# A fused attention and MLP kernel: more row transposes on SyncE's DMA queue, and the schedule around them shifted

## The chip, the cores and the metric

The kernel runs on one core of a Trainium2 chip. The metric is the device time of one execution in microseconds (us); lower is better. Three executions of the kernel before are given, and one more was profiled.

## The reference, cut to what matters

Eight batches, eight heads each, 576 positions, head width 64. Per head: causal attention with a decay bias that comes from a running sum over the positions. Then, per batch, the heads are laid side by side (512 columns), normalised and sent through an MLP with a residual.

```python
scores = q @ k.T / 8                              # causal, 576 x 576 per head
bias   = -(cum[:, None] - cum[None, :])           # cum = cumsum(max(s, 0))
attn   = softmax(where(causal, scores + minimum(bias, 0), -1e9))
x      = concat_heads(attn @ v)                   # (8, 576, 512)
xn     = (x - mean(x)) / sqrt(var(x) + 1e-6) * g_ln
out    = x + maximum(xn @ w_ch1, 0) @ w_ch2       # 512 -> 2048 -> 512
```

## The kernel before

**Order by hand.** Every engine executes its instructions in the order in which the program issues them. Batch 0 and the first heads of the next two batches follow a written plan (a long word list, not touched). From head 18 on a loop runs over the remaining heads: n counts all 64 heads, b = n // 8 is the batch, h = n % 8 the head in the batch.

**One head n.** `scores(b, h)` issues the score matmuls in three PSUM banks (sa, sb, sc; line 346), each followed by an exponential on ScalarE; GpSimd clears the part above the diagonal (line 366). Every second head adds the small last block (`scores_d`, line 382). `pv_next()` does attention times V (line 424) for the head issued two heads earlier, and VectorE normalises it.

**MLP units as filler.** Between these steps TensorE gets units of the MLP of the batch before, taken from the list `queue`. A chunk is one batch's MLP over 512 rows: 16 units of `mlp1` (line 538, four 128x512 matmuls each) and 16 of `mlp2` (line 556, the same size), 32 in all. A chunk ends at a fixed head (`end`), where the rest of the list is run and the next batch's 32 units are put in; its first unit is then issued behind the next head's scores. The number of units in a head is the rest of the list divided by the heads left. The fourth unit of each block of 128 rows is followed by VectorE's residual add (`yo`, line 565) and a store issued by SyncE (line 583).

**Rows of x.** In the heads h = 1 and 2 of batch b, `ln_xn` makes the normalised rows `xn` of batch b-1 on VectorE: four tiles of 128 rows, and for odd batches a fifth one that holds the 64 last rows of two batches. The MLP needs them transposed (xT, xTm). For b up to `NXD` = 6 that is done by `ln_tr` in the heads 2 and 3: four TensorE transposes per tile (line 526) into PSUM and a copy by VectorE or ScalarE. For b = 7 and at the end `ln_tr_dma` does it: one DMA transpose per tile, issued by SyncE (line 518).

**Rows of q and k.** A group `gam` is four heads; the even groups are the heads 0 to 3 of a batch, the odd ones 4 to 7. From group 5 on its k and q are loaded in five tiles of rows: two loads per tile issued by SyncE (`ld_rows`, line 175, into a staging pool of six), a cast with the bias columns on GpSimd (`cast_rows`, lines 192 and 195), and a DMA transpose per tile issued by SyncE (`tr_rows`, line 208) into one of two buffers `kq`. `pre(n)` and `post(n)` place these steps by m = n - 4 gam: loads at m = -6, -5, -4, casts at -5, -4, -3, transposes at -4 (tiles 0, 1) and -3 (tiles 2, 3, 4). The group's first scores are at m = 0.

**One queue.** All of SyncE's transfers stand in one order: stores, loads, transposes. An issue waits in that order for what it needs (the store for `yo`, a transpose for its cast or for `xn`), and everything behind it waits too.

Of the kernel before, what the change touches and what calls it, by code (L numbers as in the profile page):

```python
# [19 lines left out]
def kernel(  # L20
# [11 lines left out]
    nc = tc.nc  # L32
    B, H, S, D = q.shape
# [13 lines left out]
    G = 4  # L47
    NG = BH // G
    NPE = 5
    NM = 10  # L50
    NHW = 16
    NXD = 6
    KT = 96
    QT = 6
    QP = S // QT
# [103 lines left out]
    def ld_cast_pair(g):  # L159
        ld_cast("k", g)  # L160
        ld_cast("q", g)

    def ld_cast_v(b, t):
        pn = P if t < NF else TL
        nc.gpsimd.dma_start(  # L165
            out=v_bf[b % 2][:pn, t, :, 0:D],
            in_=v[b, :, t * P : t * P + pn, :].rearrange("h s d -> s h d"),
        )

    def ld_rows(gam, t):  # L170
        pn = P if t < NF else TL
        b, h0 = gam // 2, (gam % 2) * G
        tmp = stage.tile([P, 2, G, D], F32, name="rowtmp", tag="st")
        for u, src in enumerate((k, q)):
            nc.sync.dma_start(  # L175
                out=tmp[0:pn, u],
                in_=src[b, h0 : h0 + G, t * P : t * P + pn, :].rearrange("h s d -> s h d"),
            )
        loaded["rows", gam, t] = tmp

    def ld_cast_rows(gam, t):
        pn = P if t < NF else TL
        b, h0 = gam // 2, (gam % 2) * G
        for u, src in enumerate((k, q)):
            nc.gpsimd.dma_start(
                out=rows[t][0:pn, u, :, 0:D],
                in_=src[b, h0 : h0 + G, t * P : t * P + pn, :].rearrange("h s d -> s h d"),
            )
# [10 lines left out]
    def bias_of_rows(gam, t):  # L199
        pn = P if t < NF else TL  # L200
        nc.vector.tensor_copy(
            out=rows[t][0:pn, :, :, D:KA], in_=cT[0:pn, t, :, gam * G : (gam + 1) * G, :]
        )

    def tr_rows(gam, t):
        pn = P if t < NF else TL
        o = t * 2 * G * P
        nc.sync.dma_start_transpose(
            out=kq[home(gam)]
            .rearrange("p u h s -> p (u h s)")[:, o : o + 2 * G * pn]  # L210
            .rearrange("p (h s) -> p h s", s=pn),
            in_=rows[t][0:pn].rearrange("p u h c -> p (u h c)"),
        )
# [8 lines left out]
    def ld_w2(i):  # L222
        nc.gpsimd.dma_start(
            out=w2_bf[:, 4 * i : 4 * i + 4, :], in_=w2_r[:, 4 * i : 4 * i + 4, :]
        )
# [3 lines left out]
    def aug(gam, eng, h0=0):  # L229
        r = slice(gam * G + h0, gam * G + G)  # L230
        i = home(gam)
        eng.dma_start(out=kq[i][D : D + 1, 1, h0:G, 0:S], in_=c_hi[r, :])
        for j in range(3):
            eng.dma_start(out=kq[i][D + 1 + j : D + 2 + j, 0, h0:G, 0:S], in_=c3[r, j, :])
# [214 lines left out]
    def x_tiles(b):  # L449
        ts_ = [xb[b][:, t, :] for t in range(NF)]  # L450
        if b % 2 == 1:
            ts_.append(xm[b // 2])
        return ts_

    st = {}

    def ln_stats(b, part):
        if part == 0:
            st[b] = small.tile([P, 5, 3, 6], F32, name="stats", tag="stats", bufs=2)
        lo, hi = ((0, 256), (256, 384), (384, 512))[part]  # L460
        for t, x in enumerate(x_tiles(b)):
            nc.vector.bn_stats(out=st[b][:, t, part, :], in_=x[:, lo:hi])  # L462

# [8 lines left out]
    def ln_rstd(b):  # L474
        n = len(x_tiles(b))
        rs = rstd[:, b, 0:n]
        nc.vector.tensor_scalar_add(out=rs, in0=mvs[b][:, 0:n, 1], scalar1=1e-6)  # L477
        nc.gpsimd.tensor_tensor(out=rs, in0=rs, in1=mhalf[:, 0:n], op=ALU.pow)  # L478

    def ln_aggr(b, t):  # L480
        nc.vector.bn_aggr(out=mvs[b][:, t, :], in_=st[b][:, t, 0 : 2 if b == 0 else 3, :])

    def ln_xn(b, t):
        tiles = x_tiles(b)
        if t >= len(tiles):
            return
        if b == 0:
            nc.vector.tensor_scalar(
                out=mean0[:, t : t + 1],
                in0=sum0[:, t, 0:1],  # L490
                scalar1=sum0[:, t, 1:2],
                scalar2=1.0 / Dm,
                op0=ALU.add,
                op1=ALU.mult,
            )
        else:
            ln_aggr(b, t)
        xn = xnp.tile([P, Dm], BF16, name="xn", tag="xn")
        nc.vector.scalar_tensor_tensor(  # L499
            out=xn,  # L500
            in0=tiles[t],
            scalar=mvs[b][:, t, 0:1] if b > 0 else mean0[:, t : t + 1],
            in1=gb,
            op0=ALU.subtract,
            op1=ALU.mult,
        )
        xns[b, t] = xn
        if b > 0 and t == len(tiles) - 1:
            ln_rstd(b)

    def xT_dst(b, t):
        if t < NF:
            return xTs[b][:, :, t * P : (t + 1) * P]
        return xTm[:, :, (b // 2) * P : (b // 2 + 1) * P]

    def ln_tr_dma(b, t):
        if (b, t) in xns:
            nc.sync.dma_start_transpose(out=xT_dst(b, t), in_=xns.pop((b, t)))
# [78 lines left out]
    def run_units(n, dve_first=False):  # L597
        for i in range(n):
            if queue:
                first_unit[0] = dve_first and i == 0  # L600
                queue.pop(0)()

# [25 lines left out]
    for i in range(2):  # L630
# [8 lines left out]
        out=maskT,  # L639
        in_=maskT,  # L640
# [210 lines left out]


    def pre(n):
        if n in PAIR_LOADS:
            ld_cast_pair(PAIR_LOADS[n])
        if n in (11, 12):
            ld_w2(n - 9)
        if n in (8, 9):
            aug(n - 5, nc.sync)
        for gam in range(NPE, NG):  # L860
            m = n - 4 * gam
            ts_ = {-6: (0, 1), -5: (2, 3), -4: (4,)}.get(m, ())
            for t in ts_:
                if gam < NHW:
                    ld_rows(gam, t)
                else:
                    ld_cast_rows(gam, t)
                    bias_of_rows(gam, t)
            if gam >= NHW:
                for t in {-4: (0, 1), -3: (2, 3, 4)}.get(m, ()):  # L870
                    tr_rows(gam, t)
        for nb in range(2, B):
            t = n - H * nb + {2: 5, 3: 4}.get(nb, 6)
            if 0 <= t < NT:
                ld_cast_v(nb, t)

    def post(n):
        for gam in range(NPE, NHW):
            m = n - 4 * gam
            for t in {-4: (0, 1), -3: (2, 3)}.get(m, ()):  # L880
                tr_rows(gam, t)
            for t in {-5: (0, 1), -4: (2, 3), -3: (4,)}.get(m, ()):
                cast_rows(gam, t)
            if m == -3:
                tr_rows(gam, 4)

    def pv_next():
# [5 lines left out]
        if ph_ == 7:  # L893
# [6 lines left out]
            out=c_in[:, 0:P], in0=c_in[:, 0:P], scalar=0.0, in1=eight, op0=ALU.max, op1=ALU.mult  # L900
# [24 lines left out]
            out=c_in[:, P:S], in_=c_in[:, P:S], func=ACT.Relu, scale=1.0 / scale  # L925
# [44 lines left out]
    for word in PLAN.split():  # L970
        step, _, eng = word.partition(":")
# [2 lines left out]
        STEPS[name](*args, *([E[eng]] if eng else []))  # L974

    pend += [(2, 0), (2, 1)]
    FIRST = {24: 2}
    for n in range(2 * H + 2, BH):
        b, h = n // H, n % H
        pre(n)  # L980

        end = next(m for m in [8 * i + (3 if i <= NXD else 4) for i in range(2, B)] + [BH + 3] if m >= n)
        nu = -(-len(queue) // (end - n + 1)) - 2
        if n in FIRST:
            run_units(FIRST[n])
            nu -= FIRST[n]
        scores(b, h)
        run_units(1, True)
        if h % 2 == 0:
            scores_d(b, h // 2)  # L990
        post(n)
        run_units(1)
        pv_next()
        pend.append((b, h))
        if b <= NXD:
            if n == 2 * H + 2:
                for t in range(3, NT):
                    ln_xn(1, t)
            for t in {1: (0, 1, 2), 2: (3, 4)}.get(h, ()) if b > 2 else ():
                ln_xn(b - 1, t)  # L1000
                if t in (1, 2, 4):
                    run_units(1)
                    nu -= 1
            for t in {2: (0, 1), 3: (2, 3, 4)}.get(h, ()):
                ln_tr(b - 1, t, "act" if b == 2 else "dve")
                if t not in (1, 4) and nu > 0:
                    run_units(1)
                    nu -= 1
        elif h in (1, 2):
            for t in ((0, 1, 2), (3, 4))[h - 1]:  # L1010
                ln_xn(b - 1, t)
                ln_tr_dma(b - 1, t)
                run_units(1)
                nu -= 1
        run_units(nu)
        if n == end:
            run_units(len(queue))
            queue += batch_units(b - 1)
# [41 lines left out]
```

## Time and profile before

| | us |
|---|---|
| three executions: median (lowest, highest) | 357.67 (356.28, 358.16) |
| the profiled execution: its time | 357.56 |
| its span, first to last instruction | 355.8 |
| TensorE busy in the span | 347.7 (98%) |
| VectorE, ScalarE, GpSimd busy | 197.1, 185.6, 161.9 |
| mean granted TensorE clock | 1.000 |

The profiled execution lies 0.11 us under the median, and 1.8 us of its time lie outside the span. A line of the profile's groups reads: line of the kernel, engine, operation, written and read tiles and shape, count | busy time in us, mean ns of one | idle time of the engine just before, and what ended it. SPq rows are what SyncE issues; their duration is the time that the issue took, not the transfer. "<-" stands between what is written and what is read.

### The profile page before, as it was taken

Reading aid. Unit: us, or ns where it says so; the run is one execution under the profiler, and the core shown is the slowest. Engines: PE = TensorE matmul, PEld = TensorE weight load, DVE = VectorE, ACT = ScalarE, POOL = GpSimd, SP = SyncE. Lnnn points to the kernel's source line nnn. Section 1 sums busy time; section 2 is a strip of 40 time slices with the busy share of each in tenths; the row PEclk is TensorE's granted clock in tenths of the full one; section 3 lists DMA queues with packets and bytes.
Section 4 is the critical chain, followed back from the end, with each engine's and each line's share of the span. In section 5 each row is a group of like instructions: output and inputs, shape, how many; then the busy total and the mean of one; then the engine's idle time right before and its main releaser. Section 6 shows DMA issues by size and latency. Waiting matters only on the chain.

```text
span 355.8 us, 8451 instructions
## 1 busy us (share of the span) xinstructions
PE 347.7 (98%) x3170; PEld 199.3 (56%) x3170; DVE 197.1 (55%) x535; ACT 185.6 (52%) x359; POOL 161.9 (45%) x340
## 2 busy tenths in 40 slices
PE   7999998999999999999999999999999999999995
PEld 3899665555555555655555555555555544444444
DVE  7788877854277545944385548643664492113112
ACT  4899785577633773267435752476356502502500
POOL 9996578367366535583547354845341000000000
PEclk9999999999999999999999999999999999999999
DMA  9999999999999998799599958999650033011013
GB/s 150 173 172 161 202 192 171 160 223 162 179 189 199 175 210 113 156 209 186 112 189 182 198 117 150 216 173 175 133 129 2 0 73 121 0 61 60 0 32 89
DMA packets 169258, 49.73 MB, mean 140 GB/s; under 512 B 157776, under 2 KB 164608, under 8 KB 169216
## 3 DMA queue, kind: packets, MB, share of 16 engines
q1 hardware_dynamic: 116096, 36.53, 54.4%
q0 software_dynamic: 51600, 11.87, 37.4%
q10 hardware_dynamic: 1520, 0.79, 0.9%
q8 instruction: 25, 0.41, 0.5%
q14 instruction: 17, 0.14, 0.1%
HBM read 37.11 MB, written 9.44 MB: 131 GB/s over the span
## 4 chain that ended last, share of the span: by engine, by line
PE 83%; DMA 9%; SPq 3%; DVE 2%; ACT 2%; issue 0%; POOL 0%; DVEq 0%
PE py L556 31%; PE ph L538 31%; PE pot L424 6%; DMA v_bf<-in_v_dram 4%; PE sc L346 3%; PE sb L346 3%; PE sa L346 3%; DMA rowtmp<-in_k_dram 3%; SPq L175 3%; DMA kq<-c 2%; PE trx L526 2%; PE st L716 1%; ACT er L733 1%; PE trt L694 1%; DMA out_dram<-yo 1%
## 5 line engine op out<-in xcount | busy, mean ns | idle before, releaser
L556 PE MATMUL py<-w_bf,hT 128*128 128x512 bf16 (+2 forms) x608 | 135.6, 368 | 1.2 <-DMA w_bf<-in_moe_w_ch_dram 1.2
L538 PE MATMUL ph<-xT,w_bf 128*128 128x512 bf16 x480 | 113.3, 379 | 0.0
L548 ACT ACTIVATE hT<-ph 128x512 bf16<-128x512 f32 x101 | 60.2, 598 | 73.1 <-PE ph L538 73.1
L556 PEld LDWEIGHTS <-hT 128*128 128x128 bf16 x608 | 53.9, 98 | 51.3 <-issue 1.3
L366 POOL TENSOR_SCALAR_AFFINE_SELECT er<-er 128x256 bf16<-128x256 bf16 x108 | 44.9, 423 | 81.8 <-ACT er L357 80.8
L538 PEld LDWEIGHTS <-w_bf 128*128 128x128 bf16 x544 | 48.9, 98 | 49.2
L357 ACT ACTIVATE er<-sa 128x512 bf16<-128x512 f32 x56 | 33.4, 596 | 63.8 <-PE sa L346 47.7
L546 DVE TENSOR_SCALAR hT<-ph 128x512 bf16<-128x512 f32 x35 | 24.2, 692 | 56.6 <-PE ph L538 51.6
L346 PEld LDWEIGHTS <-kq 68*128 68x128 bf16 x412 | 29.5, 97 | 20.3
L424 PEld LDWEIGHTS <-er 128*128 128x128 bf16 x840 | 32.9, 98 | 12.4 <-issue 0.5
L565 DVE SCALAR_TENSOR_TENSOR yo<-py,rstd,xb 128x512 f32<-128x512 f32 x32 | 24.0, 749 | 28.6 <-PE py L556 20.6
L192 POOL CAST kq<-rowtmp 128x512 bf16<-128x512 f32 (+1 forms) x55 | 33.3, 606 | 8.7 <-DMA rowtmp<-in_q_dram 8.2
L424 PE MATMUL pot<-v_bf,er 128*128 128x65 bf16 x840 | 35.3, 193 | 0.5 <-DMA v_bf<-in_v_dram 0.4
L436 DVE RECIPROCAL rinv<-pot 128x5 f32<-128x5 f32 x56 | 10.7, 191 | 44.4 <-PE pot L424 44.3
L165 POOL DMA_DIRECT2D v_bf<-in_v_dram x40 | 34.5, 870 | 0.5 <-ACT er L357 0.3
L357 ACT ACTIVATE er<-sc 128x512 bf16<-128x512 f32 x56 | 34.2, 610 | 0.0
L357 ACT ACTIVATE er<-sb 128x512 bf16<-128x512 f32 x56 | 33.5, 598 | 0.0
L438 DVE TENSOR_TENSOR xb<-pot,rinv 128x256 f32<-128x256 f32 x56 | 23.8, 425 | 1.9
L478 POOL TENSOR_TENSOR rstd<-rstd,mhalf 128x4 f32<-128x4 f32 (+1 forms) x8 | 8.9, 1112 | 34.3 <-DVE rstd L477 34.3
L499 DVE SCALAR_TENSOR_TENSOR xn<-xb,mv,gb 128x512 bf16<-128x512 f32 x28 | 22.4, 800 | 1.0
L462 DVE BATCH_NORM_STATS2 stats<-xb 128x6 f32<-128x128 f32 (+1 forms) x84 | 21.9, 320 | 0.3
L346 PE MATMUL sc<-kq 68*128 68x256 bf16 (+1 forms) x200 | 21.7, 226 | 0.1
(115 smaller groups left out, 352.0 us busy)
## 6 DMA issues: line engine op xcount, KB each, us to landing
out_dram<-yo SPq DMA_DIRECT2D x32, 256.0 KB
rowtmp<-in_k_dram SPq DMA_DIRECT2D x44, 128.0 KB
rowtmp<-in_q_dram SPq DMA_DIRECT2D x44, 128.0 KB
v_bf<-in_v_dram POOLq DMA_DIRECT2D x32, 128.0 KB, 5.7
w_bf<-in_moe_w_ch_dram POOLq DMA_DIRECT2D x8, 512.0 KB, 10.2
kq<-kq SPq DMA_TRANSPOSE x55
kp<-in_k_dram POOLq DMA_DIRECT2D x6, 144.0 KB, 9.5
qp<-in_q_dram POOLq DMA_DIRECT2D x6, 144.0 KB, 9.4
```

The costliest lines, as they stand in the source:

```text
L165: nc.gpsimd.dma_start(out=v_bf[b % 2][:pn, t, :, 0:D], in_=v[b, :, t * P : t * P + pn, :].rearrange("h s d -> s h d"),)
L192: nc.gpsimd.tensor_copy(out=rows[t][0:pn, :, :, 0:D], in_=loaded.pop(("rows", gam, t))[0:pn])
L346: nc.tensor.matmul(a[:, c + a0 - q0 : c + a1 - q0], lhsT=k_cols(b, h, kb), rhs=cols, start=True, stop=not (pe_mask and diag),)
L357: nc.scalar.activation(out=e[:, o : o + 512], in_=a, func=ACT.Exp, scale=scale)
L366: nc.gpsimd.affine_select(out=two, in_=two, compare_op=ALU.is_ge, fill=0.0, base=0, pattern=[[0, 2], [1, P]], channel_multiplier=-1,)
L424: nc.tensor.matmul(pot[:, t, :], lhsT=e[:, o : o + P], rhs=vv[:, kb, h, :], start=(kb == 0), stop=(kb == last),)
L438: nc.vector.tensor_tensor(out=xb[b][:, :, hs], in0=pot[:, 0:NF, 0:D], in1=rinv[:, 0:NF].unsqueeze(2).to_broadcast([P, NF, D]), op=ALU.mult,)
L538: nc.tensor.matmul(ph, lhsT=w1_bf[:, kd, fb * P : (fb + 1) * P], rhs=xT[:, kd, :], start=(kd == 0), stop=(kd == KD - 1),)
L546: nc.vector.tensor_scalar_max(out=hT[:, fb, :], in0=ph, scalar1=0.0)
L548: nc.scalar.activation(out=hT[:, fb, :], in_=ph, func=ACT.Relu)
L556: nc.tensor.matmul(py[t], lhsT=hT[:, fb, t * P : (t + 1) * P], rhs=w2_bf[:, fb, c0:c1], start=(fb == 0), stop=(fb == FB - 1),)
L565: nc.vector.scalar_tensor_tensor(out=yo, in0=py[t], scalar=rs, in1=x[:, c0:c1], op0=ALU.mult, op1=ALU.add)
```

## The change

Six things are changed together:

1. `NXD` is 2 instead of 6: the rows of the batches 2 to 5 (18 tiles) are transposed by SyncE's DMA, no longer by TensorE. In the DMA branch the steps are placed anew: tiles 0 and 1 are transposed in head 1, tiles 2 and 3 in head 2, the fifth in head 4.
2. By the same constant, the chunks of these batches end one head later (h = 4), so a new chunk begins in the fifth-numbered head, h = 5. In the loop the long chunk of nine heads is now the one in the heads 20 to 28 instead of the one in the heads 52 to 60.
3. The row steps of the even groups from 6 on (loads, casts, transposes of q and k) are placed one head later.
4. In every head with h = 0 or 4 from head 24 on, two MLP units are issued ahead of the scores; before, that was so in head 24 alone.
5. VectorE's statistics (`bn_stats`) are no longer issued in one block but two behind each MLP unit; the rest of them at the last part, ahead of their use.
6. Two of GpSimd's loads move: the third and fourth quarter of `w_ch2` are both issued in head 11 ahead of the pair load (before: heads 11 and 12, behind it), and batch 3's V is loaded in the heads 18 to 22 instead of 20 to 24.

```diff
-    NXD = 6
+    NXD = 2
...
+    todo = []
+
+    def run_todo(n):
+        for _ in range(min(n, len(todo))):
+            todo.pop(0)()
...
         for t, x in enumerate(x_tiles(b)):
-            nc.vector.bn_stats(out=st[b][:, t, part, :], in_=x[:, lo:hi])
+            todo.append(
+                lambda t=t, x=x: nc.vector.bn_stats(out=st[b][:, t, part, :], in_=x[:, lo:hi])
+            )
+        if part == 2 or b < 2:
+            run_todo(len(todo))
...
                 queue.pop(0)()
+                run_todo(2)
...
     def pre(n):
+        if n == 11:
+            ld_w2(2)
+            ld_w2(3)
         if n in PAIR_LOADS:
             ld_cast_pair(PAIR_LOADS[n])
-        if n in (11, 12):
-            ld_w2(n - 9)
...
         for gam in range(NPE, NG):
-            m = n - 4 * gam
+            m = n - 4 * gam - (gam % 2 == 0 and gam > NPE)
...
-            t = n - H * nb + {2: 5, 3: 4}.get(nb, 6)
+            t = n - H * nb + (5 if nb == 2 else 6)
...
     def post(n):
         for gam in range(NPE, NHW):
-            m = n - 4 * gam
+            m = n - 4 * gam - (gam % 2 == 0 and gam > NPE)
...
-    FIRST = {24: 2}
+    XN_AT = {1: ((0, 1, 2), (0, 1)), 2: ((3, 4), (2, 3)), 4: ((), (4,))}
...
         end = next(m for m in [8 * i + (3 if i <= NXD else 4) for i in range(2, B)] + [BH + 3] if m >= n)
         nu = -(-len(queue) // (end - n + 1)) - 2
-        if n in FIRST:
-            run_units(FIRST[n])
-            nu -= FIRST[n]
+        if h % G == 0 and n > 4 * NPE:
+            run_units(2)
+            nu -= 2
         scores(b, h)
...
-        elif h in (1, 2):
-            for t in ((0, 1, 2), (3, 4))[h - 1]:
+        elif h in XN_AT:
+            for t in XN_AT[h][0]:
                 ln_xn(b - 1, t)
+                if t != 1 and nu > 0:
+                    run_units(1)
+                    nu -= 1
+            for t in XN_AT[h][1]:
                 ln_tr_dma(b - 1, t)
-                run_units(1)
-                nu -= 1
```

## The prediction

> **What bounds the kernel now.** I read the page's busy rows first.
>
> ```profile
> PE 347.7 (98%) x3170; PEld 199.3 (56%) x3170; DVE 197.1 (55%) x535; ACT 185.6 (52%) x359; POOL 161.9 (45%) x340
> ...
> PE   7999998999999999999999999999999999999995
> ...
> PEclk9999999999999999999999999999999999999999
> DMA  9999999999999998799599958999650033011013
> ```
>
> TensorE is busy in every slice at the full clock; nobody else comes near. The list of waits shows what it still waits for behind the start: 1.2 us once for `w_ch2`, 0.4 us once for V.
>
> ```profile
> PE py L556 <- DMA w_bf<-in_moe_w_ch_dram: 1.2, 1, 1.2
> PE pot L424 <- DMA v_bf<-in_v_dram: 0.4, 1, 0.4
> ```
>
> From 70 us on the chain of waits is TensorE alone. So work taken from TensorE shortens the run, as long as nothing else comes late. The next suspect is SyncE's queue. Its timeline in batch 5:
>
> ```profile
> 189.57 0.36 SPq L583 DMA_DIRECT2D out_dram<-yo  x1
> 189.97 0.63 SPq L175 DMA_DIRECT2D rowtmp<-in_k_dram  x1
> 190.64 1.75 SPq L175 DMA_DIRECT2D rowtmp<-in_q_dram  x1
> 192.52 7.47 SPq L208 DMA_TRANSPOSE kq<-kq  x5
> 200.04 0.58 SPq L175 DMA_DIRECT2D rowtmp<-in_k_dram  x1
> 200.68 0.52 SPq L175 DMA_DIRECT2D rowtmp<-in_q_dram  x1
> ```
>
> A plain load takes 0.55 us of this queue, a q/k row transpose 1.4. Per batch: 20 loads 12.0, ten transposes 15.4, four stores 1.6, together 29.0 of 37.95 us (head 44's first unit at 189.25 to head 52's at 227.20).
>
> **The transposes on TensorE (a gain).** The groups and TensorE's timeline:
>
> ```profile
> L526 PE MATMUL trx<-ident,xn 128*128 128x128 bf16 x108 | 10.3, 219 | 0.0
> L116 DVE COPY xT<-trx 128x512 bf16<-128x512 bf16 x18 | 7.1, 415 | 0.1
> ```
> ```profile
> 219.11 1.03 PE L556 MATMUL py<-w_bf,hT 128*128 128x512 bf16 x4
> 219.98 0.39 PE L526 MATMUL trx<-ident,xn 128*128 128x128 bf16 x4
> 220.20 1.03 PE L556 MATMUL py<-w_bf,hT 128*128 128x512 bf16 x4
> 221.06 0.39 PE L526 MATMUL trx<-ident,xn 128*128 128x128 bf16 x4
> 221.29 0.38 PE L346 MATMUL sa<-kq 68*128 68x512 bf16 x1
> ```
>
> 219 ns is the time of one through the pipeline; what it takes of the stream is the step from one start to the next: four transposes move the next matmul by 0.22 us (219.98 to 220.20), a unit takes 0.87. 18 tiles x 0.22 = 4.0 us, all on the path. The 18 copies (0.415 us each, most on VectorE) go too; VectorE is not on the path, so 0.
>
> [...]
>
> **What comes onto SyncE.** 18 issues; the rows there are (batches 6 and 7) show the price:
>
> ```profile
> L518 SPq DMA_TRANSPOSE xT<-xn x8: 1189/1220/1890, 255.2 to 293.1; - x8
> ```
>
> With the step between issues 1.31 us: 5.2 us in a batch with four tiles, 6.6 with five. The queue's sum becomes 34.2 to 35.6 of a period that falls to 37.0 (37.95 less 4.5 x 0.22). It still fits, but it is nearly full. By the semaphore arrivals in the trace these eight land up to 3.3 us behind the end of their issue. The DMA engines have room where they fall, in heads 1 and 2: their share is 0.62 at 206 to 216 us and 0.79 at 216 to 224, against 1.28 and 1.47 in the next 20 us.
>
> [...]
>
> Are the new xT in time? In batch 3 (nine-head chunk): head 25 starts at 98.2 as before, its first `xn` is done some 5.6 us later (head 49: 211.63 to 217.67, 6.0; head 25 has a unit less), so two issues from 103.9 to 106.5, a store, the third to 108.6, and the fourth behind the last `xn` to 109.9; landed by 112.6 with 2.7 us. The first unit that reads it is behind head 29's scores, about 113.85 (before, head 29 began at 117.54; less four units of 0.87 and four tiles of 0.22, plus 0.65 for the scores). 1.2 us early; in later batches some 3 us early.
>
> **The even groups a head later (the cost).** Behind a chunk's last store comes a fixed run of issues, and group 8's, 10's, 12's, 14's last row transpose must land before the second score bank of heads 32, 40, 48, 56. Let T be the first score of the h = 4 head. The chunk now ends in this head: two units ahead of T, then scores 0.65, unit 0.87, small block 0.07, unit 0.87, `yo` 0.75, 0.3 to the issue: the last store goes at T + 3.5. Behind it: store 0.4; two loads 1.2; two transposes; four loads of the next odd group 2.2 (new here; before they came behind all five); three transposes; then the landing of the last. In batches 4 and 6 one xTm, 1.31, stands ahead.
>
> Five transposes took 8.47, 8.12, 7.47, 8.97 us in the four batches before (mean 8.26), where single issues swelled to 2.3 to 2.96; five undisturbed ones at 1.4 are 7.0. I take 7.8: nearer the measured ones, with four loads between that let the queue drain. The last one landed 1.55 to 4.50 us behind its issue over ten groups; I take 2.85. Sum: 3.5 + 0.4 + 1.2 + 7.8 + 2.2 + 2.85 = T + 17.95. The need: T to the next h = 0 head's first score was 18.40 (188.59 to 206.99), and both heads have two units ahead now; the second bank is 0.22 later: T + 18.6. So 0.65 early (head 48); with xTm 0.65 late (40 and 56). Head 32 follows the nine-head chunk, whose heads 25 to 28 have three units, not four: its need is T + 17.8, SyncE reaches the store at T + 3.65, and it is 0.25 late. Together 0.25 + 0.65 + 0.65 = 1.55; 0.45 more for the scatter of the landings, which only counts when late: **2.0 us of new waiting**. Bounds: with 7.0 nobody is late (0); with 8.97 and a landing of 4.25 the four are 2.4 to 3.7 late, 13 together.
>
> [...]
>
> Group 6 (head 24) landed at 91.2 for a need at 95.5; with a head of delay and four loads ahead about 93.5, still early. What is queued behind these waits on SyncE is the odd group's loads; that group now is ready some 7 us ahead of its scores (before: 221.90 for 226.54), since the first store no longer stands between its transposes.
>
> **Edits with little in them.** Two units ahead of the scores: the same units, moved; they are the 1.73 us in the needs above. Chunk a head later: same work; from head 61 on both kernels agree. The statistics in twos: 96 the same instructions on an engine 55% busy; 0. `w_ch2` earlier: the 1.2 us wait at 60.4 goes, but the next wait is V at 69.04, on GpSimd's same queue with the same bytes ahead of it, so TensorE only comes there earlier and waits longer; 0 to 1.2, I take 0. Batch 3's V two heads earlier: needed in head 26, never waited for; 0, or 0.5 either way by loading the 62 to 80 us stretch.
>
> **Sum.** 357.56 - 4.0 + 2.0 = 355.56, with the median 0.11 above the profiled time: **355.6 us**.
>
> **Rivals.** (1) Nobody is late: the five take 7.0, and up to 1.2 of the wait for `w_ch2` goes: 352.4 to 353.6. For it: the added loads between let the queue drain. Against: three of four batches before showed swollen issues. Chance 0.13. (2) Slower: SyncE's run to the even groups swells as it did at 229 us (8.97, landing 3 to 4.25), and each of heads 32, 40, 48, 56 waits 1.5 to 2.5 us: 6 to 10 us against 4.0: 359.5 to 363.5. It decides from about 1.0 us of mean lateness per boundary, where the gain is gone. For it: a queue 93 to 96% full, more transfers in flight. Against: V's loads compete for fewer of these heads. Chance 0.24. (3) No change to speak of: the xT of batch 3 come late by 1 us and the even groups eat 3: 357.5. Chance 0.13. The forecast's own case, 353.6 to 357, has 0.50.
>
> Over 0.5% (1.8 us, about what a measurement of this kernel can tell from no change; the three runs span 0.5%) faster means under 355.8. That is rival 1 and about two thirds of the forecast's case: 0.47. Slower means over 359.4: 0.23 from rival 2. The rest, 0.30, is within. Range 353.0 to 360.5: a tenth below (the lower half of rival 1), a tenth above (the upper half of rival 2).
>
> **What the profile would show.** Right: 36 transposes left on TensorE instead of 108, 24 DMA transposes of xT and three of xTm; TensorE's waits at kq in the scores of heads 32, 40, 56, 0.3 to 1.5 us each. Wrong on the gain: TensorE's chain shorter by something other than 4.0. Wrong on the cost: no wait at kq, or waits of over 2 us; a wait at a chunk's first `mlp1` speaks for rival 3; a wait for V at about 69 us that is as long as before would mean that `w_ch2` did pay.

## The result and the profile after: 4.2% slower

The changed kernel takes 371.89 us (median of four executions, 371.63 to 376.06); the kernel before took 357.41 beside it. The ratio is 1.042, 95% interval 1.036 to 1.047. The profiled execution of the changed kernel is one of 372.14 us with a span of 370.4; before it was 357.56 and 355.8. So 14.6 us have to be found. The forecast was 355.6, the range ended at 360.5, and none of the cases weighed reached 364. All medians here are over every execution, while the ratios leave out those over 1.5% above the fastest of their kernel (three of e3's ten, one each of e5's, e6's and e11's, and one of the kernel before's).

The page of the changed kernel, in the rows of which those of before were shown:

```profile
PE 351.4 (95%) x3098; PEld 197.2 (53%) x3098; DVE 190.8 (52%) x517; ACT 187.4 (51%) x359; POOL 162.4 (44%) x340
...
PE   8999999999998989996999999897999999999995
...
PEclk9999999999999999998899999997899999999999
DMA  9999999999999999999869999999550015002013
```

TensorE has 72 matmuls less and yet is busy 3.7 us longer. Its row now has holes in the middle of the run, and behind the two deepest the clock row drops too; the row of before shows no such drop. The list of waits says what the holes wait for (columns: us in total, times, longest):

```profile
PEld L346 <- DMA kq<-kq: 4.5, 5, 2.1
...
PE sa L346 <- issue: 3.7, 2, 2.3
...
PE sa L346 <- DMA kq<-kq: 3.3, 1, 3.3
...
PE ph L547 <- DMA xT<-xn: 2.8, 2, 1.8
...
PE sb L346 <- DMA kq<-kq: 1.2, 4, 0.4
```

All are first scores of an even group and first units of a chunk. By heads, from TensorE's timeline: 1.76 us for xT at head 29, 1.79 at head 32, 3.49 at head 40, 0.40 at head 48, 1.00 for xT at head 53, 2.49 at head 56 (both score banks added). The two scores put down to "issue" are those of heads 32 and 56; there it is the weight load of the same kq that waits, the PEld row. Together 10.9 us.

The clock comes on top. The stretch around head 40's wait in four windows of 3.41 us (columns: window, its length, TensorE busy with its matmuls, granted clock, DMA share, GB/s; the DMA share takes the whole time of every packet that began in the window, so it can be over 1):

```profile
169.03:172.44 3.41, 1.06 (x5) 1.00 1.01 192
172.44:175.86 3.42, 2.27 (x11) 0.50 0.75 159
175.86:179.27 3.41, 3.41 (x23) 0.50 0.86 178
179.27:182.68 3.41, 3.41 (x40) 1.00 1.03 196
```

Behind the wait the clock is 0.50 for 6.83 us; a second such stretch, 254.36 to 261.19, lies behind head 56's wait. Of these 13.66 us TensorE is busy for 12.31 (the first stretch began inside the wait, the second has short gaps); half of that, some 6.2 us, is lost to the clock, an estimate from the busy time and from the step of a unit there, 1.69 us (175.02 to 176.71) against 0.87 at full clock.

**The account.** I summed TensorE's steps, from one matmul's start to the next's, over the heads 16 to 63: 218.1 us before, 230.6 after. The transposes' steps went from 5.14 to 1.11, a gain of 4.03. Waits went from 1.70 to 10.95, a loss of 9.25. All other steps grew by 7.3: some 6.2 for the half clock, and 1.1 that I did not tell apart. -4.03 + 9.25 + 7.3 = 12.5. The other 2.1 us were lost in the heads 8 to 15, nearly all to short waits: 1.1 for V at head 9 and 0.7 at head 12 for a block that GpSimd clears. Inside the sum they are balanced by the 1.7 us of waits for `w_ch2` and V that the heads 17 and 18 had before and that went away.

**Where SyncE stood.** Its timeline in batch 4; T, the first score of head 36, is 151.52:

```profile
145.03 0.38 SPq L592 DMA_DIRECT2D out_dram<-yo  x1
145.50 2.54 SPq L527 DMA_TRANSPOSE xT<-xn  x2
...
148.77 2.51 SPq L527 DMA_TRANSPOSE xT<-xn  x2
...
153.65 2.06 SPq L592 DMA_DIRECT2D out_dram<-yo  x1
...
158.60 0.83 SPq L592 DMA_DIRECT2D out_dram<-yo  x1
159.47 1.22 SPq L527 DMA_TRANSPOSE xTm<-xn  x1
```

The last store goes at 158.60, T + 7.1 where the sum had T + 3.5. It does not wait for its `yo` then; SyncE is still busy with what stands ahead: from the first xT on, four transposes, two stores and eight loads of the shifted group, 13.1 us with one gap of 0.3. The prediction worked its start out for batch 3 alone: the end of the first `xn`, 5.6 us behind the head's start. Here that would be 141.6 (the first `xn` ends at 142.04), but the run starts at 145.5, because a store stands ahead of it. VectorE's timeline at that place:

```profile
141.29 0.75 DVE L508 SCALAR_TENSOR_TENSOR xn<-xb,mv,gb 128x512 bf16<-128x512 f32 x1
...
143.34 0.87 DVE L508 SCALAR_TENSOR_TENSOR xn<-xb,mv,gb 128x512 bf16<-128x512 f32 x1
144.25 0.75 DVE L574 SCALAR_TENSOR_TENSOR yo<-py,rstd,xb 128x512 f32<-128x512 f32 x1
```

TensorE has finished the unit of this `yo` at about 140.6, but VectorE does three `xn` first; the store, and both transposes behind it, wait for that. In the other chunks the last store went at T + 6.7 (head 28), 4.7 (44) and 6.6 (52).

### The profile page after: what moved, and what is told of

It reads as the page before. It is cut to its first block, busy times and chain, and to the rows that moved or that the text cites. A ratio compares the mean times of both kernels' runs of the same rounds, so it can differ in the third digit from the quotient of the medians.

```text
span 370.4 us, 8334 instructions
## 1 busy us (share of the span) xinstructions
PE 351.4 (95%) x3098; PEld 197.2 (53%) x3098; DVE 190.8 (52%) x517; ACT 187.4 (51%) x359; POOL 162.4 (44%) x340
## 4 chain that ended last, share of the span: by engine, by line
PE 54%; DMA 19%; POOL 8%; SPq 7%; DVE 6%; issue 4%; ACT 0%; POOLq 0%; DVEq 0%; ACTq 0%
PE py L565 24%; PE ph L547 17%; DMA rowtmp<-in_q_dram 9%; DMA kq<-kq 4%; PE pot L424 4%; SPq L175 3%; DMA kp<-in_k_dram 3%; SPq L527 3%; PE sb L346 2%; DMA v_bf<-in_v_dram 2%; POOL er L366 2%; PE sc L346 2%; PE sa L346 2%; POOL v_bf L165 1%; DVE yo L574 1%
## 5 line engine op out<-in xcount | busy, mean ns | idle before, releaser
L565 PE MATMUL py<-w_bf,hT 128*128 128x512 bf16 (+2 forms) x608 | 133.8, 368 | 0.0
L547 PE MATMUL ph<-xT,w_bf 128*128 128x512 bf16 x480 | 116.2, 387 | 2.8 <-DMA xT<-xn 2.8
L547 PEld LDWEIGHTS <-w_bf 128*128 128x128 bf16 x544 | 49.9, 99 | 54.4 <-issue 4.1
L424 PEld LDWEIGHTS <-er 128*128 128x128 bf16 x840 | 33.7, 99 | 13.7 <-issue 1.5
L346 PE MATMUL sa<-kq 68*128 68x512 bf16 x56 | 21.9, 392 | 7.0 <-issue 3.7
L436 DVE RECIPROCAL rinv<-pot 128x5 f32<-128x5 f32 x56 | 10.7, 191 | 33.6 <-PE pot L424 33.5
L346 PE MATMUL sb<-kq 68*128 68x64 bf16 (+1 forms) x156 | 22.1, 247 | 1.3 <-DMA kq<-kq 1.2
## 6 DMA issues: line engine op xcount, KB each, us to landing
w_bf<-in_moe_w_ch_dram POOLq DMA_DIRECT2D x8, 512.0 KB, 10.8
qp<-in_q_dram POOLq DMA_DIRECT2D x6, 144.0 KB, 10.4
```

The source lines that it names most:

```text
L346: nc.tensor.matmul(a[:, c + a0 - q0 : c + a1 - q0], lhsT=k_cols(b, h, kb), rhs=cols, start=True, stop=not (pe_mask and diag),)
L424: nc.tensor.matmul(pot[:, t, :], lhsT=e[:, o : o + P], rhs=vv[:, kb, h, :], start=(kb == 0), stop=(kb == last),)
L547: nc.tensor.matmul(ph, lhsT=w1_bf[:, kd, fb * P : (fb + 1) * P], rhs=xT[:, kd, :], start=(kd == 0), stop=(kd == KD - 1),)
L565: nc.tensor.matmul(py[t], lhsT=hT[:, fb, t * P : (t + 1) * P], rhs=w2_bf[:, fb, c0:c1], start=(fb == 0), stop=(fb == FB - 1),)
```

## The experiments

Each is the changed kernel with the edit shown, unless said otherwise, timed beside the kernel before; e9 to e12 stand in the text alone. T is always the first score of the h = 4 head of a chunk, in whose own timeline the times are read.

| run | us (median) | ratio to before, 95% | last store of the four chunks at T + |
|---|---|---|---|
| changed | 371.9 | 1.036 to 1.047 | 6.7, 7.1, 4.7, 6.6 |
| e1: 18 tiles on TensorE | 359.1 | 1.000 to 1.006 | 1.0, 4.2, 3.4, 3.4 |
| e14: e1 with tiny copies | 360.5 | 1.006 to 1.009 | 4.6, 4.7, 3.9, 3.6 |
| e15: e1 with scratch transposes | 369.8 | 1.029 to 1.038 | 5.8, 5.6, 5.3, 4.9 |
| e4: units before xn | 366.5 | 1.018 to 1.028 | 6.6, 4.8, 5.2, 6.2 |
| e2: groups not shifted | 364.9 | 1.014 to 1.025 | 7.8, 10.7, 9.7, 10.8 |
| e3: four units ahead | 362.5 | 1.007 to 1.014 | not given |
| e7: e4 and e3 | 361.4 | 1.005 to 1.016 | 6.9, 6.1, 5.1, 5.7 |
| e6: loads by GpSimd | 363.4 | 1.008 to 1.016 | 4.6, 4.6, 3.4, 3.4 |
| e5: e4 and e6 | 360.7 | 1.001 to 1.008 | 3.9, 3.4, 3.4, 3.4 |
| e13: e3, e4, e6; 14 tiles | 358.0 | 1.000 to 1.003 | 1.0, 3.4, 3.4, 3.4 |

**e1, the transposes back on TensorE.** The rest is as changed, except that the old branch brings its own places of the MLP units around the rows with it.

```diff
-        if b <= NXD:
+        if b <= 6:
```

> The changed kernel with the 18 tiles of xn of the batches 2 to 5 transposed on TensorE again (as before the change); chunk ends, the even groups' rows a head later, two units ahead and everything else stay as changed. Theory A (SyncE's queue is late because of the 18 issues and of the stores and xn they wait for): SyncE reaches a chunk's last store by about T+3.5 to T+4.5 (T: first score of the h = 4 head) instead of T+4.65 to T+7.1, no wait for kq over 0.5 us at heads 32, 40, 48, 56, no half-clock stretch; 372.1 - 10.9 (gaps) - 6.8 (half clock) + 4.0 (transposes) = about 358.4, at most 360. Rival B (the head-later shift alone makes the rows late): waits of 1 us and more stay at heads 32, 40, 48, 56 and the time is over 362.

Measured 359.1. The waits at kq shrink to 0.67 us at head 40 and 0.19 at head 20, and the clock stays up. So the 18 DMA transposes are worth +12.8 us (371.9 less 359.1) instead of -2.0, the forecast's -4.0 + 2.0; the other edits, together 1.6 us over before, bring nothing by themselves. Not all of the 12.8 need be the queue's: by the branch's places of the units the last store of batch 3's chunk goes at T + 1.0 in e1, as it did before. The wait for `w_ch2` did pass to V, as the prediction had it: 1.27 us at 67.6.

**e14 and e15: which property of the 18 transposes.** Both are e1 with 18 extra transfers of `xn` to a scratch tile that nobody reads, at the places of SyncE's order where the change has its transposes.

The copy in e14, and the transpose in e15 (`xkeep` holds the `xn` tiles):

```diff
+        nc.sync.dma_start(out=scr[0:1, t % 2], in_=xkeep[b, t][0:1, :])
```
```diff
+        nc.sync.dma_start_transpose(out=scr[:, t % 2], in_=xkeep[b, t])
```

> The changed kernel with the 18 tiles of batches 2 to 5 transposed on TensorE again (as in e1), and in SyncE's order, where the change has its 18 DMA transposes, 18 plain copies of one row of xn (1 KB each) into a scratch tile that nobody reads. They wait for xn as the transposes do, but take some 0.4 us of issue instead of 1.25. Theory A1 (the issue time counts): the queue gains 18 x 0.4 = 7 us over the whole run instead of 22, the last store goes at T + 3.4 to 4.5, waits at kq of 0 to 1.5 us in all: 359 to 361.5 us (e1: 359.1). Theory A2 (the place in the order counts: what waits for xn and stands behind a late yo holds all that follows): last store at T + 5 to 7, waits at kq as in the changed kernel, 364 to 372 us.

> As e14, but with 18 full DMA transposes of xn into the scratch tile: SyncE's order, issue time and bytes as in the changed kernel, while TensorE does not use the result and keeps its own 4.0 us of transposes. By A1, A2 and by bytes alike: waits at kq of 4 to 8 us in all at heads 32, 40, 48, 56, half clock behind some, 364 to 374 us; no waits for xT. If it stays under 361 us, the SyncE queue is not the cause at all, and the changed kernel's loss comes from xT's own landings.

The issues of the two, from their line (min/median/max in ns, first and last start):

```profile
L530 SPq DMA_DIRECT2D scr<-xn x18: 497/556/2172, 106.3 to 232.2; - x18
```
```profile
L530 SPq DMA_TRANSPOSE scr<-xn x18: 1188/1226/2204, 106.4 to 238.7; - x18
```

And e15's waits:

```profile
PE sa L346 <- DMA kq<-kq: 3.4, 3, 2.0
PE sa L346 <- issue: 3.1, 2, 1.8
...
PE sb L346 <- DMA kq<-kq: 1.1, 3, 0.6
```

The place in the order and the wait for `xn` alone (e14) cost 1.4 us; the last stores go 1.2 us later than in e1 on average, and the waits at kq are 2.4 us. The full transposes move the last stores by another 1.2 us, and the waits to 7.2 us: 9.3 us more, of which up to 3.4 come from two stretches of 3.41 us at half clock in the profiled execution. Together that is 10.7 us over e1 with the MLP units in the same places, so most of the 12.8 is the queue's. So theory A1 holds, though e14's waits and two of its last stores are a little over what it allowed: most of the loss comes with the transposes' size, their 1.23 us of issue against 0.56, and little with what they wait for. Issue time and bytes go together in e15, and no run here takes them fully apart. Their bytes do not show in the time from the last store to the last landing: 14.2 to 15.5 us in e14, 13.9 to 15.9 in e15, 14.5 to 16.2 in the changed kernel.

**e4, units before the rows.** The head's MLP units are issued ahead of the `xn` of heads 1 and 2, so that VectorE makes `yo` first.

```diff
         elif h in XN_AT:
+            if XN_AT[h][0] and nu > 0:
+                run_units(nu)
+                nu = 0
             for t in XN_AT[h][0]:
                 ln_xn(b - 1, t)
-                if t != 1 and nu > 0:
-                    run_units(1)
-                    nu -= 1
```

> The changed kernel with the rest of a head's MLP units issued ahead of the xn in heads 1 and 2, so that VectorE does the residual add (yo) before the three xn and SyncE's first store no longer waits behind them. Theory A: the first store of a chunk goes out some 3 us earlier, the last store about 2 us earlier, the waits for kq at heads 32, 40, 56 shrink by 1 to 2 us each and one or both half-clock stretches go: 361 to 367. Rival: the queue is full by its sum of issues alone, the xT come no earlier than before; 370 to 373.

Measured 366.5. The first store goes 2.0 us earlier in batches 4 and 6 and 2.8 in batch 5, and the last 2.3 and 0.4 us earlier in batches 4 and 6, but 0.5 later in batch 5 and as late as before the edit in batch 3. Of the 5.4 us won, the waits at kq give 1.0 (8.2 to 7.2; head 40 gives 1.2, head 56 takes 0.5), the waits for xT 1.8, and one of the half-clock stretches is shorter by half. So `yo` behind `xn` is a part of the lateness, not the whole.

**e2, the even groups not shifted** (`- (gam % 2 == 0 and gam > NPE)` taken out in both places).

> The changed kernel with the row steps of the even groups placed where they were (a head earlier). Theory A: the same number of issues, but four loads move ahead of two xT transposes and the four odd-group loads move behind the even group's last transposes; the waits for kq at heads 32, 40, 48, 56 fall under 0.5 us, the waits for xT at the chunk starts (heads 29, 37, 45, 53; 1.8 and 1.0 us and none and none in the changed kernel) grow to 1.5 to 3 us each; no or one half-clock stretch; 360 to 367. Rival C (the DMA engines are full, place does not matter): waits for kq stay at 1 us and more, time 369 or more. Rival B (the shift alone is the fault): no waits of either kind, 354 to 356.

Measured 364.9: 7 us better than the changed kernel, and as expected a different loss. Now the xT are late, by 3.4 us at head 29, 2.7 at 37 and 1.4 at 53, since four of the even group's loads stand ahead of the last two of them in head 2, and TensorE waits for kq only 1.3 us at head 56. (The last stores of three chunks go at T + 9.7 to 10.8, but there the group's transposes stand ahead of them.) The shift buys timely xT with late kq; SyncE has no room for both.

**e3, four units ahead of the scores in heads 32, 40, 48, 56, and e7, the same with e4.**

```diff
+        four = h == 0 and n >= 32
         if h % G == 0 and n > 4 * NPE:
-            run_units(2)
+            run_units(4 if four else 2)
```

(The two units that stood behind these heads' scores are not issued again.)

> The changed kernel with all four MLP units of the heads 32, 40, 48, 56 ahead of their scores, not two. Theory A with the clock following the length of the wait: the waits for kq (1.8, 3.5, 0.4, 2.5 us) shrink by 1.73 each to 0, 1.8, 0, 0.8; none is long enough for a half-clock stretch or one is; 372.1 - 5.6 - (3.4 to 6.8) = 360 to 363. Rival D (the half-clock stretches come from the kernel's load, not from the waits): both stay; about 366.5.

> The changed kernel with the units ahead of the normalised rows in heads 1 and 2 (e4) and four units ahead of the scores in heads 32, 40, 48, 56 (e3). Four units ahead move the need by 1.73 us; e4's waits were 1.6, 1.8, 0.2 and 2.5 us. Theory A (the waits are lateness against a fixed need): 0, 0 to 0.4, 0, 0.8 are left, and the wait for xT at head 29 of about 1 us; no wait reaches 2 us and no stretch at half clock follows: 355.5 to 359.5 us. Rival (the lateness follows TensorE, because stores and rows come from it, so a later need is met by later rows): waits over 4 us in all, 362 us or more.

Measured 362.5 and 361.4. In e3, 1.73 us more for kq at each of four heads can shorten these waits by 5.6 us in all, and 10.2 us come off the changed kernel (371.9 to 361.6, the median of the seven executions that the ratio counts): a late row costs more than its lateness. (e3's profiled execution took 367.3 us, 4.9 over its median, so no times of stores stand in the table for it.) e7 has no half clock in its profile and waits 0.63 + 0.20 us at head 56, as the first theory said; but 0.79 + 0.42 at head 40, where at most 0.4 was expected, and 2.72 us for xT at head 29, more than in the changed kernel, where 1 was expected. Neither theory was right: the time lies between them.

**e6 and e5, SyncE relieved of loads.** The tiles 2, 3 and 4 of the even groups from 8 on are loaded by GpSimd with a cast on the way; e5 adds e4's edit.

```diff
+    def by_pool(gam, t):
+        return gam % 2 == 0 and gam > 6 and t >= 2
...
-                if gam < NHW:
+                if gam < NHW and not by_pool(gam, t):
                     ld_rows(gam, t)
                 else:
                     ld_cast_rows(gam, t)
                     bias_of_rows(gam, t)
```

> The changed kernel with the GpSimd loads alone (tiles 2, 3 and 4 of the even groups from 8 on), the order of rows and units as changed. Theory A: about 1.1 us less of queue in the run behind each last store and less in the run ahead of it, so of the waits of 1.4, 3.3, 0.4 and 2.3 us at heads 32, 40, 48, 56 about 2 us or less is left in all, the waits for xT at heads 29 and 53 (1.8 and 1.0) stay within 1 us of what they were: 358 to 364 us. Theory B: as the changed kernel, 369 to 373 us.

> The changed kernel with two edits: in heads 1 and 2 the head's MLP units come ahead of the normalised rows (as in the run e4), and the tiles 2, 3 and 4 of every even group from 8 on are loaded by GpSimd with a casting load instead of SyncE's two loads and GpSimd's cast; six loads of some 0.55 us each, 3.3 us per batch, leave SyncE's queue, two of them from the stretch between a chunk's last store and the even group's last transpose. Theory A (SyncE's queue is overfilled by the time its issues take, so every relief of it counts): the waits at heads 32, 40, 48, 56 fall from 6 us in e4 to under 1.5 us in all, no stretch at half clock, 354 to 359 us. Theory B (not the issues but the DMA engines' load makes the rows late, and a load that moves to another queue moves nothing): waits at kq of 4 us or more stay, 363 to 367 us.

Measured 363.4 and 360.7. With six loads less per batch SyncE is at three of the four last stores at T + 3.43 in e5 (two of four in e6): the T + 3.5 of the prediction, with SyncE now waiting there for `yo`. In e5's batch 4, where T is 150.77, VectorE makes the last `yo` as soon as TensorE has finished it, and the second of the two stores of SyncE's line goes at 154.20:

```profile
153.43 0.75 DVE L574 SCALAR_TENSOR_TENSOR yo<-py,rstd,xb 128x512 f32<-128x512 f32 x1 [3.14 <-PE py L565]
```
```profile
151.27 3.29 SPq L592 DMA_DIRECT2D out_dram<-yo  x2
```

The term was right for a queue that has room, and it is the room that was missing. e6 also speaks for the issues and against the bytes: the same rows are still loaded, by another queue, and the last stores go 1.2 to 3.1 us earlier. But theory A's 1.5 us of waits in e5 became 3.9, and its time, 354 to 359, was missed; in e6 its 2 us became 4.7, with 2.4 more at head 24. From the first to the last of the five transposes of kq it now takes 12.2 to 13.5 us instead of 10.4 to 11.1; GpSimd's loads of a full tile take 5.1 and 5.2 us to land by the median, and some of these transposes presumably stand behind them, which no run separates.

**e9, one late group in the kernel before.** The row steps of group 10 alone two heads later, so that TensorE waits once (the edit stands in `pre` and in `post`).

```diff
-            m = n - 4 * gam
+            m = n - 4 * gam - 2 * (gam == 10)
```

> The kernel before with one edit: the row steps of group 10 alone (heads 40 to 43) two heads later. Its last transposes are then issued about 9 us later than before and must make TensorE wait once, some 4 to 7 us at head 40. Theory C (a wait of over some 2 us is followed by 3.4 or 6.8 us at half the clock, each costing half its length): wait plus 3.4, 365 to 368 us, with one stretch of 6.8 us at a granted clock of 0.5 directly behind it. Rival (the half clock in the changed kernel has another cause, and a wait costs only its own length): 361.5 to 364.5 us, clock 1.000 throughout.

Head 40's first score waits 4.4 us. In windows of the profiled execution (TensorE, weight loads, VectorE, ScalarE and GpSimd busy, then clock, DMA share, GB/s):

```profile
170.40:173.80 3.40, 0.00 (x0) 0.00 (x0) 0.00 (x0) 0.08 (x1) 0.00 (x0) 1.00 1.01 197
173.80:180.60 6.80, 6.26 (x35) 3.07 (x36) 0.23 (x2) 1.85 (x4) 2.53 (x7) 0.50 0.57 108
```

This execution took 365.8 us, 8.2 over the profiled one before: 4.4 of wait, some 3.1 for the half clock (half of the 6.26 busy us), and some 1 us more of the early waits for `w_ch2` and V. The median of the four is 364.0, in the rival's range, but their mean clocks are 0.990 to 0.995, never 1.000: in two of them 0.995 speaks for half the stretch. (The mean clock alone would not prove it: five of the 61 executions of the kernel before beside these runs have 0.993 or 0.994 too.) In the profiled execution theory C is seen at work, with a price of up to 1.7 or up to 3.4 us.

**e10, e11, e12: the transposes on ScalarE's queue.** In e11 they are moved to places where `xn` should be done; e12 is e11 without the shift of the even groups.

```diff
-            nc.sync.dma_start_transpose(out=xT_dst(b, t), in_=xns.pop((b, t)))
+            (nc.scalar if b < 7 else nc.sync).dma_start_transpose(out=xT_dst(b, t), in_=xns.pop((b, t)))
```

> The changed kernel with one edit: the DMA transposes of xn to xT and xTm (batches 2 to 6) are issued by ScalarE instead of SyncE, at the same places in the program. The same transfers load the DMA engines; only the queue differs. Theory A (SyncE's own order and issue time make the rows late): the last store goes at T + 3.4 to 4, no wait at kq over 0.7 us at heads 32, 40, 48, 56, and the time falls by 10 us or more to 354 to 361 us; ScalarE may wait for xn and hold exponentials back, which costs 0 to 4 of these. Theory B (the DMA engines' load makes the rows late): the waits at kq stay, 4 us or more in all, 366 us or more.

> As the run before it, with ScalarE's issues placed where xn is long done: tile 0 at the end of head 1, tiles 1 and 2 at the end of head 2, tile 3 in head 3 behind its exponentials. If ScalarE's waiting for xn cost anything there, it goes: no waits of TensorE over 0.7 us. The run with 18 tiles on TensorE had 359.1 us; less the 4.0 us of TensorE's transposes that is 355, and 353.5 to 357 is expected by theory A; theory B 366 or more.

> As e11, and the even groups' row steps where they were before the change. If the shift of the even groups is only there to make room for SyncE's xT transposes, then without these it is not needed: the groups' transposes stand ahead of the last store again, no wait at kq, 353 to 356 us. If the chunk that ends a head later needs the shift (its stores stand ahead of the transposes' loads), waits at kq of 0.5 to 2 us each come back: 357 to 362 us.

Measured 381.1, 372.3 and 377.3: both theories missed the time. The waits at the heads 32, 40, 48 and 56 were indeed gone in e10, the last stores at T + 2.5 to 3.4. A new wait took their place. ScalarE's timeline in e10:

```profile
109.02 2.62 ACTq L527 DMA_TRANSPOSE xT<-xn  x2
111.73 0.60 ACT L357 ACTIVATE er<-sa 128x512 bf16<-128x512 f32 x1 [10.52 <-DMA rowtmp<-in_k_dram]
```

ScalarE does nothing for 7.8 us ahead of its first transpose (its exponential before ends at 101.2), and the exponential behind comes after 10.5; TensorE then waits 5.85 us for ScalarE at head 27 and about 3 at the heads 35, 43 and 51. Of the 27 semaphore instructions that line 527 has on ScalarE's queue the longest lasts 7.59 us, the median 0.04, and the profile puts the end of the 10.52 us down to the landing of a load of k that SyncE issued; what holds the first transpose back was not shown. As TensorE came late by then, the missing kq waits say little about SyncE, and the test of the queue fell to e14 and e15.

**e13, an attempt at a faster version.** e3, e4 and e6 together, and batch 2's rows, which came late at head 29, on TensorE.

```diff
-        if b <= NXD:
+        if b <= NXD + 1:
```

> An attempt at a faster version: units ahead of the normalised rows, tiles 2, 3 and 4 of the even groups from 8 on loaded by GpSimd, four units ahead of the scores in heads 32, 40, 48, 56 (e4, e6 and e3 together), and batch 2's rows, the ones that came late at head 29, transposed on TensorE as before, so 14 tiles instead of 18 leave TensorE: 14 x 0.22 = 3.1 us. e5 had 360.7 us with waits of 1.0 at head 29 and 3.9 at the heads 32, 40, 56 (both banks); four units ahead move the need by 1.73 us, which covers each of these. Theory A: 360.7 - 1.0 - 3.9 + 0.9 = 356.7, between 355 and 358.5, level with the kernel before or up to 2.5 us under it. Rival (the rows follow TensorE's time, as part of the lateness did in e7): 359 to 362 us.

Measured 358.0 (twelve executions), ratio 1.000 to 1.003: the loss is gone and nothing is won. The clock stays full, and the waits at kq are 1.0 us at head 40, 0.6 at head 24 and 0.35 at head 20. The 3.1 us taken from TensorE are spent on these, on 1.6 us of short waits in the heads 9 to 12, and on the scores, whose steps for the banks sa and sb, without the waits named, grew from 20.6 to some 22.5 us over the heads 16 to 63.

## Why the prediction was wrong, point by point

- **The gain: right.** 4.0 us predicted, 4.03 measured in TensorE's steps; 36 transposes left, 24 DMA transposes of xT and three of xTm, as forecast.

```profile
L535 PE MATMUL trx<-ident,xn 128*128 128x128 bf16 x36 | 3.3, 219 | 0.0
```
```profile
L527 SPq DMA_TRANSPOSE xT<-xn x24: 1192/1220/2230, 105.5 to 307.0; - x24
```

- **The price of an issue: right** (1.22 us). The run behind the last store, 14.45 and 15.76 with xTm to the last landing, was right in its sum: 15.1, 15.5, 14.5, 16.2 measured. In part that is luck: from the first of the five transposes to the end of the last, with the four loads between, it took 10.4 to 11.1 us instead of 10.0, and the last landed 1.6 us behind that instead of 2.85.
- **The step that failed: "the last store goes at T + 3.5".** It was worked out from when `yo` would be ready, as if SyncE stood there waiting. SyncE came at T + 6.7, 7.1, 4.7 and 6.6, 2.8 us later on average, and the waits at kq were 8.2 us instead of 2.0. The prediction did add up the queue for a batch, 34.2 to 35.6 us of 37.0, and let "it still fits" stand for "it is in time": a sum over a period says nothing of the order inside it. In batch 4, 13.1 us of issues stand from the first xT to the last store. Had the first xT gone at the end of its `xn`, as the prediction had it for batch 3 (here head 33's 136.0 + 5.6 = 141.6), they would have ended at T + 3.2, with nothing to spare; it went at 145.5, because the store ahead of it waits for a `yo` that VectorE makes after three `xn`, and the run had only 0.3 us of waiting in it to make up for that. Issues that swelled, one to 2.06 us, are in the 13.1. e15 against e14 shows that the size of the transposes makes most of the loss, e4 that the late start is a part, and e5 that the term holds once the queue has room.
- **A cost not in the sum at all: the clock.** Some 6 us beside 8.2 of waits at kq, and more than the whole gain. At the forecast's own lateness, under 0.7 us at each head, it would not have come, by the counts of the last section. Of the 16.3 us between forecast and result, 6.2 are thus waits at kq beyond the forecast's 2.0, 2.8 waits for xT, some 6 the clock, and the rest small steps and waits.
- **xT in time: wrong at head 29**, where "1.2 us early" became 1.76 late, the landing at 115.99 instead of 112.6; the first xT was issued at 105.5 instead of 103.9, behind three transposes of an odd group that the prediction had left out there; the first `xn` was done at 104.17.

```profile
101.37 4.04 SPq L208 DMA_TRANSPOSE kq<-kq  x3
105.50 3.75 SPq L527 DMA_TRANSPOSE xT<-xn  x2
```

  The first two xT then took 3.75 us instead of 2.6, and the last landed 3.5 us behind the end of its issue instead of 2.7. Wrong too at head 53 (1.0 late, 3 early predicted): the first xT went behind a store that waited for `yo`, as in batch 4, and the last landed 4.5 us behind the end of its issue.
- **Group 6: 2.3 us later than said.** It landed at 95.8, not at 93.5, for head 24's first score at 95.4. That costs next to nothing here; in e5, e6 and e13 TensorE waits 0.6 to 2.4 us there.
- **The rivals.** Rival 2 named the heads and the price, 6 to 10 us (8.2 measured), but for another reason: a run behind the last store that swells. That run was as forecast, and the lateness came ahead of it, so its 6 to 10 is luck as far as the reason goes. It stopped at 363.5 because it had neither the clock nor, beside it, the late xT of rival 3 (1 us there, 2.8 measured). The two were kept apart as alternatives, although one full queue makes both. Its sum has a slip that nothing rests on: the upper bound of 2.4 to 3.7 us late, 13 together, adds the 0.45 of scatter to each head; the terms as named give 1.9 to 3.2, 11 together.
- **Edits at nothing: right within 1.6 us**, what e1 leaves for all of them together; none was run alone. `w_ch2`'s wait went and came back at V or in the heads 9 to 12; the 0.7 us at head 12 for GpSimd, which the kernel before does not have, may come from moving `w_ch2`, and no run separates it. The statistics and batch 3's V do not show.

## What to carry to other kernels

A queue that is 95% full by its sum has to be walked in order, from the first issue that is added to the one that a deadline hangs on, and each issue that waits for a product of another engine taken at the time when that engine makes it. And where a transfer can come late, price the wait with what follows it: here the waits of 3.5 us at head 40 and 2.5 at head 56 were each followed by 6.83 us at half clock, which cost, by the estimate above, some 3 us more each time.

## What the runs showed of the hardware

The half-clock stretches lie on a grid. In each profiled execution all their starts and ends within the run lie on one grid of 3.41 us: 172.44, 179.27, 254.36 and 261.19 above, in the changed kernel, are 2 and 24 steps apart (6.83 and 81.92 us). I counted TensorE's idle time in each cell of this grid in fifteen profiled kernels, start and end of the run left out. All fifteen cells (at full clock) with 1.95 us of idleness or more were followed by 3.41 or 6.83 us at half clock; of seven with 1.59 to 1.94 four were; below that none was. Among them are 2.35 and 2.30 us in the changed kernel (cells from 169.03 and 250.94) and 3.40 in e9 (from 170.40), each followed by 6.8 us at half clock, and 1.95 in e15 (from 128.57), followed by 3.41; 1.72 in the changed kernel (from 114.41) was followed by none. So in these runs a half-clock stretch goes with about half a cell of idleness, and not with the wait's length. e7 shows it best: its wait of 2.72 us at head 29 falls across a border, 0.78 us in one cell and 1.94 in the next, and the clock stays at 1.00 (columns: TensorE busy, clock, DMA share, GB/s).

```profile
111.08:114.49 3.41, 2.64 (x37) 1.00 3.37 122
114.49:117.91 3.42, 1.47 (x7) 1.00 1.52 213
```

In e6, whose profiled execution has a mean clock of 0.994, 1.64 us at head 40, within one cell, were followed by 3.41 us at half clock. So in these runs a gap from 1.6 us on could cost clock, and the gap of 2.29 us ahead of head 56 was followed by as long a stretch at half clock (6.83 us) as that of 3.29 at head 40.
